# Loading the later groups' queries and keys once, two heads on 128 partitions, with the split parts written across the halves

## The chip, the cores and the metric

The kernel runs on one core of a Trainium2 chip. The metric is device microseconds of one execution, the median of several runs.

## What is computed

Causal attention with a bias that decays with the cumulated `s`, then two expert layers on its output. Cut to what matters:

```python
scores = q @ k.T / sqrt(D)                       # B, H, S, D = 2, 8, 576, 64
cum = cumsum(maximum(s, 0))
scores = where(causal, -1e9, scores + minimum(-(cum[:, None] - cum[None, :]), 0))
x = softmax(scores) @ v                          # -> 1152 tokens of 512
h = x @ w_in                                     # 512 x 2048
x = where(h > 0, h, exp(minimum(h, 0)) - 1) @ w_out
out = sum_e p[:, e] * (maximum(x @ w1[e], 0) @ w2[e])   # 4 experts, 512 x 1024
```

Everything is float32 outside. Inside, products that must be exact are made of rounded numbers (float32r): a number is split into a high part (a rounded copy, made by ScalarE) and a low part (the number less its high part, made by VectorE), and three products or, in the attention, two stacked ones give the full result.

## The kernel before

The engines are TensorE (PE), VectorE (DVE), ScalarE (ACT), GpSimd (POOL) and SyncE (SP), which issues the loads. The 1152 tokens are worked in three groups (`GROUPS`) of 256, 448 and 448 tokens. For each group there is attention, the first layer (`layer1`, 16 weight units) and the second layer (4 experts of 8 units). The attention of group 0 (`attention_first`) comes first by itself; that of groups 1 and 2 (`attention_parts`) is cut into small parts which run as `background` between the slots of the layers of the group before: group 1's beside the last slots of group 0's first layer (from slot `BG_FROM[0]`, 14) and all of its second layer, group 2's beside group 1's first layer.

A slot of the first layer (`up1`, `down1`) makes `up` products of one unit, an `e` on ACT (L721, L724), a `gt` on DVE (L725) and, two slots later, the `acc` products with it. There are two `up` buffers, so a slot's `up` products wait for the `gt` of two slots before. At the end of group 0's first layer ACT rounds the four sums to `yh` (L772), and the second layer begins with products of `yh` and `yl`.

The weights of the first layer come coded and are decoded on ACT and DVE in `decode_halves` (L150, L157, L158, L160), 32 halves; POOL writes each decoded unit to `w_dec` (L163), from which groups 1 and 2 read it again. The weights from unit 16 on are loaded into `raw` (`fetch`, L97, three buffers) and split by `prepare`: a cast on ACT (L103) and a subtraction on DVE (`split_lo`, L87). Units are numbered here in this order: unit 16 is the first of the second layer of group 0.

A job of `attention_parts` is one pair of heads (128 rows of `qT` and `kT`) with its query chunks. Group 1 has four small jobs (128 queries, batch 1), loaded together by `load_small` into one tile `pt`, and four of 320 queries and 576 keys; group 2 has four of 256 queries and 384 keys and four of 192 queries and 576 keys. These are loaded by `load`. An item is one 128-query chunk of one head. Its two products (`qk`) are

```python
PE.matmul(pss, job[j, "q"], job[j, "kh"], start=True, stop=False)    # [q high; q low] x [k high; k high]
PE.matmul(pss, job[j, "qb"], job[j, "kl"], start=False, stop=True)   # [q high; bias rows] x [k low; bias rows]
```

so `qs` and `kh` need 128 partitions of one head whose width is 64. Before, each head was therefore loaded twice, onto partitions 0 to 63 and onto 64 to 127 (`for half in range(2)`, L420 to 422 and L442 to 447), and `split` copies 128 partitions to `qs` (L478) and `kh` (L479) and lets DVE overwrite the upper half of `qs` with the low part. Chunks of 64 queries (`j is None`) take both heads at once with rows `64 * jj` of `q` and `k` (L497).

The code gives the order in which work is recorded; the framework's scheduler then fixes, when the program is built, the order on each engine, and each engine works through its own in order. Loads of the first jobs are held until the last coded half is issued (`late`). SP uses eight completion semaphores in turn, so that a load is issued once the eighth before it has landed.

Of the kernel before, what the change touches and what calls it, by code (L numbers as in the profile page):

```python
# [12 lines left out]
AF = mybir.ActivationFunctionType  # L13
# [40 lines left out]
def tile_kernel(ctx, tc, qT, kT, v, s, w64, w, probs, out):  # L54
# [13 lines left out]
    PE, DVE, ACT, POOL, SP = nc.tensor, nc.vector, nc.scalar, nc.gpsimd, nc.sync  # L68
# [6 lines left out]
    def sb(shape, tag, bufs, dtype=F32):  # L75
        p = (base if tag in BASE else edge if tag in EDGE else l1_pool if tag in L1
             else att_pool[0])
        return p.tile(shape, dtype, tag=tag, name=tag, bufs=bufs)
# [7 lines left out]
    def split_lo(lo, x, hi):  # L86
        DVE.tensor_tensor(out=lo, in0=x, in1=hi.bitcast(F32), op=ALU.subtract)  # L87
# [141 lines left out]
    def cum_rows(h0, heads, n, out_):  # L229
        return dict(  # L230
            out=out_,
            in_=cum_d[h0:h0 + heads, 0:n].rearrange("(o h) k -> o h k", o=1)
            .to_broadcast([out_.shape[0], heads, n]),
        )
# [163 lines left out]
    def attention_parts(g, x):  # L398
# [3 lines left out]
        for b, chunks, col in JOBS[g]:  # L402
            cb = CHUNKS[b]
            q0, q1 = cb[chunks[0]], cb[chunks[-1] + 1]
            for hp in range(HP):
                job = dict(b=b, chunks=chunks, col=col, q0=q0, q1=q1, hp=hp)
                full = [i for i in chunks if cb[i + 1] - cb[i] == 128]
                mine = [dict(job=job, i=i, j=j) for j in range(2) for i in full]
# [5 lines left out]
        def load_small():  # L414

            b = small[0]["b"]
            t = sb([128, 2560], "pt", 2)
            q, k = (t[:, a:a + 1024].rearrange("p (h n) -> p h n", n=128) for a in (0, 1024))
            vv = t[:, 2048:].rearrange("p (c d) -> p c d", d=128)
            for t, x in ((q, qT), (k, kT)):  # L420
                for half in range(2):
                    SP.dma_start(out=t[64 * half:64 * half + 64],
                                 in_=x[b, :, 0:128].rearrange("(h d) n -> d h n", d=64))
            SP.dma_start(out=vv.rearrange("p c d -> p (c d)"), in_=v[b, 0:128])
            pt = sb([128, HP, 2, 128], "pt", 2)
            for job in small:
                hp = job["hp"]
                job["q"], job["k"] = q[:, 2 * hp:2 * hp + 2], k[:, 2 * hp:2 * hp + 2]
                job["v"] = vv[:, hp:hp + 1]
                job["pt"] = pt[:, hp].rearrange("p j (o n) -> p j o n", o=1)  # L430

        def load(job):
            b, hp, q0, q1 = job["b"], job["hp"], job["q0"], job["q1"]
            cb, nc_ = CHUNKS[b], job["chunks"][-1] + 1
            nq = q1 - q0
            r = slice(hp * 128, hp * 128 + 128)

            def buf(shape, tag):
                return sb(shape, tag, 2)

            for n, x, a, e in (("q", qT, q0, q1), ("k", kT, 0, q1)):
                job[n] = t = buf([128, 2, e - a], n + "2")  # L442
                for half in range(2):
                    SP.dma_start(
                        out=t[64 * half:64 * half + 64],
                        in_=x[b, r, a:e].rearrange("(h d) n -> d h n", h=2),
                    )
            h0 = b * H + 2 * hp
            if any(cb[i + 1] - cb[i] == 64 for i in job["chunks"]):
                job["cump"] = t = buf([128, 1, q1], "cbp")  # L450
                for j in range(2):
                    SP.dma_start(**cum_rows(h0 + j, 1, q1, t[64 * j:64 * j + 64]))
            job["v"] = buf([128, nc_, 128], "v")
            full = [i for i in range(nc_) if cb[i + 1] - cb[i] == 128]
            if full:
                SP.dma_start(
                    out=job["v"][:, full[0]:full[-1] + 1, :],
                    in_=v[b, cb[full[0]]:cb[full[-1] + 1], r].rearrange("(c p) d -> p c d", p=128),
                )
            for i in range(nc_):  # L460
                if i not in full:
                    SP.dma_start(out=job["v"][:64, i, :], in_=v[b, cb[i]:cb[i + 1], r])

        def split(it):


            job, j = it["job"], it["j"]
            if j is None or (j, "q") in job:
                return
            q, k = job["q"][:, j], job["k"][:, j]  # L470
            qs = sb([128, q.shape[-1]], "qs", 2, F32R)
            kh = sb([128, k.shape[-1]], "kh", 2, F32R)
            qb = sb([68, q.shape[-1]], "qb", 2, F32R)
            kl = sb([68, k.shape[-1]], "kl", 2, F32R)
            h = job["b"] * H + 2 * job["hp"] + j
            SP.dma_start(out=qb[64:].bitcast(F32), in_=rows_d[h, 2:6, job["q0"]:job["q1"]])
            SP.dma_start(out=kl[64:].bitcast(F32), in_=rows_d[h, 0:4, 0:job["q1"]])
            ACT.activation(qs, q, AF.Copy)  # L478
            ACT.activation(kh, k, AF.Copy)  # L479
            split_lo(qs[64:], q[64:], qs[64:])  # L480
            ACT.activation(qb[:64], q[:64], AF.Copy)
            split_lo(kl[:64], k[:64], kh[:64])
            job[j, "q"], job[j, "qb"], job[j, "kh"], job[j, "kl"] = qs, qb, kh, kl

        def qk(it, pss, a, e):
            job, i, j = it["job"], it["i"], it["j"]
            cb = CHUNKS[job["b"]]
            qs = slice(cb[i] - job["q0"], cb[i + 1] - job["q0"])
            if j is not None:
                PE.matmul(pss[:, :e - a], job[j, "q"][:, qs], job[j, "kh"][:, a:e],  # L490
                          start=True, stop=False)
                PE.matmul(pss[:, :e - a], job[j, "qb"][:, qs], job[j, "kl"][:, a:e],  # L492
                          start=False, stop=True)
                return
            for jj in range(2):
                r = slice(64 * jj, 64 * jj + 64)
                PE.matmul(pss[r, :e - a], job["q"][r, jj, qs], job["k"][r, jj, a:e],  # L497
                          start=True, stop=True)

        norm = []  # L500
# [79 lines left out]
        def start():  # L580
            with late():
                if small:
                    load_small()
                for job in jobs[:2]:
                    load(job)
            split(items[0])
# [504 lines left out]
```

## Time and profile before

| what | value |
|---|---|
| median of 3 runs (lowest, highest) | 712.02 us (711.47, 712.31) |
| span of the profiled execution, first to last instruction | 710.5 us |
| PE busy | 695.7 us (98%) |
| DVE, ACT, POOL busy | 561.8 (79%), 366.9 (52%), 17.7 us (2%) |
| mean granted clock of PE | 0.997 |
| moved by DMA | 97.00 MB, mean 137 GB/s |

For the profiled execution the profile gives its span; the median of the runs is 1.5 us more, for what lies around the span. Busy time of PE counts from a matmul's start to its modelled end, and matmuls overlap. DVE's and ACT's share is a mean over stretches that differ: ACT is busy for 35 to 41 of every 50 us up to 300 us and for 11 to 19 after 400. The DMA engines are busy all the time up to 95 us and about half the time from there to 350.

### The profile page before, as it was taken

Reading aid. Unit: us, or ns where it says so; the run is one execution under the profiler, and the core shown is the slowest. Engines: PE = TensorE matmul, PEld = TensorE weight load, DVE = VectorE, ACT = ScalarE, POOL = GpSimd, SP = SyncE. Lnnn points to the kernel's source line nnn. Section 1 sums busy time; section 2 is a strip of 40 time slices with the busy share of each in tenths; the row PEclk is TensorE's granted clock in tenths of the full one; section 3 lists DMA queues with packets and bytes.
Section 4 is the critical chain, followed back from the end, with each engine's and each line's share of the span. In section 5 each row is a group of like instructions: output and inputs, shape, how many; then the busy total and the mean of one; then the engine's idle time right before and its main releaser. Section 6 shows DMA issues by size and latency. Waiting matters only on the chain.

```text
span 710.5 us, 10311 instructions
## 1 busy us (share of the span) xinstructions
PE 695.7 (98%) x3670; PEld 594.1 (84%) x3670; DVE 561.8 (79%) x1158; ACT 366.9 (52%) x765; POOL 17.7 (2%) x40
## 2 busy tenths in 40 slices
PE   8999899999999999999999999999999999999997
PEld 7787688887878887887899988888888888888886
DVE  7798679887868988875975469988888888888765
ACT  5897679676667777666754343322222233322320
POOL 5011000000000000000000000000000000000000
PEclk9999999999999999999999999999999999999999
DMA  8999965765674553523552000111111111111002
GB/s 301 410 391 380 318 204 179 226 206 171 185 222 149 173 174 94 161 98 102 226 178 89 1 1 0 60 60 59 60 60 59 60 60 59 60 60 59 1 0 105
DMA packets 40868, 97.00 MB, mean 137 GB/s; under 512 B 4096, under 2 KB 17616, under 8 KB 40816
## 3 DMA queue, kind: packets, MB, share of 16 engines
q1 hardware_dynamic: 38288, 87.67, 37.0%
q0 software_dynamic: 2528, 8.67, 3.0%
q8 instruction: 29, 0.48, 0.3%
q14 instruction: 23, 0.19, 0.1%
HBM read 85.32 MB, written 11.01 MB: 136 GB/s over the span
## 4 chain that ended last, share of the span: by engine, by line
PE 89%; ACT 6%; DVE 2%; DMA 2%; issue 1%; POOL 0%; ACTq 0%; DVEq 0%; POOLq 0%
PE acc L614 39%; PE up L614 17%; PE att L926 11%; PE up L926 8%; PE att L569 3%; PE att L542 3%; ACT z L157 2%; ACT wu L150 2%; DMA raw<-in_w 2%; PE att L497 1%; PE att L490 1%; PE att L492 1%; PE acc L704 1%; PE att L362 1%; PE up L717 1%
## 5 line engine op out<-in xcount | busy, mean ns | idle before, releaser
L614 PE MATMUL acc<-w,h 128*128 128x512 f32 x672 | 172.0, 392 | 0.0
L614 PEld LDWEIGHTS acc<-w,h 128*128 128x128 f32 x672 | 126.1, 188 | 23.0 <-ACT h L936 0.2
L87 DVE TENSOR_TENSOR wu<-raw,wu 128x1024 fp32r<-128x1024 f32 x64 | 78.0, 1220 | 18.7 <-ACT wu L103 18.2
L614 PE MATMUL acc<-gt,wu 128*128 128x448 f32 x384 | 87.8, 372 | 0.0
L671 DVE SCALAR_TENSOR_TENSOR ox<-acc,pr,ox 128x512 f32<-128x512 f32 x105 | 78.5, 748 | 11.4 <-PE acc L614 9.1
L936 ACT ACTIVATE h<-c 128x448 fp32r<-128x448 f32 x48 | 27.4, 573 | 111.2 <-DVE c L942 111.2
L614 PEld LDWEIGHTS acc<-gt,wu 128*128 128x128 f32 x384 | 70.1, 188 | 7.8 <-issue 2.6
L103 ACT ACTIVATE wu<-raw 128x1024 fp32r<-128x1024 f32 x64 | 67.5, 1055 | 16.7 <-PE acc L614 14.5
L926 PE MATMUL att<-S,top 128*128 128x448 f32 x288 | 66.3, 365 | 0.0
L926 PEld LDWEIGHTS att<-S,top 128*128 128x128 f32 x288 | 54.0, 188 | 6.7 <-issue 0.2
L614 PE MATMUL acc<-wu,gt 128*128 128x512 f32 x192 | 56.1, 408 | 0.0
L614 PE MATMUL up<-yh,wu 128*128 128x256 f32 x256 | 53.4, 289 | 0.0
L937 DVE SCALAR_TENSOR_TENSOR h<-c,h 128x448 fp32r<-128x448 f32 x48 | 29.8, 623 | 18.7 <-ACT h L936 18.7
L614 PEld LDWEIGHTS up<-yh,wu 128*128 128x128 f32 x256 | 41.7, 189 | 3.4 <-issue 1.5
L926 PE MATMUL up<-x2a,top 128*128 128x448 f32 x192 | 44.2, 366 | 0.0
L614 PE MATMUL up<-xa,wu 128*128 128x448 f32 x192 | 43.5, 371 | 0.0
L614 PE MATMUL up<-ox,wu 128*128 128x448 f32 x192 | 41.5, 366 | 0.8 <-DVE e L729 0.8
L721 ACT ACTIVATE e<-up 128x448 f32<-128x448 f32 (+1 forms) x48 | 23.5, 489 | 34.0 <-PE up L614 30.2
L532 ACT ACTIVATE p<-p,nm 128x384 f32<-128x384 f32 (+4 forms) x56 | 34.5, 617 | 12.3 <-DVE nm L527 11.9
L926 PEld LDWEIGHTS up<-x2a,top 128*128 128x128 f32 x192 | 35.9, 188 | 4.8 <-ACT p L951 0.6
L936 ACT ACTIVATE h<-up 128x448 fp32r<-128x448 f32 x16 | 8.8, 547 | 59.5 <-PE up L926 59.5
L614 PEld LDWEIGHTS up<-ox,wu 128*128 128x128 f32 x192 | 36.0, 188 | 4.0 <-DVE e L729 1.1
(193 smaller groups left out, 1223.8 us busy)
## 6 DMA issues: line engine op xcount, KB each, us to landing
raw<-in_w SPq DMA_DIRECT2D x38, 512.0 KB
raw<-w_dec SPq DMA_DIRECT2D x32, 512.0 KB
raw<-in_w SPq DMA_DIRECT2D x16, 1024.0 KB
w_dec<-wu POOLq DMA_DIRECT2D x16, 512.0 KB, 7.4
cd<-in_w SPq DMA_DIRECT2D x9, 512.0 KB
k<-in_kT SPq DMA_DIRECT2D x16, 288.0 KB
xa<-in_w SPq DMA_DIRECT2D x5, 512.0 KB
cbp<-cum_d SPq DMA_DIRECT2D x16, 144.0 KB
```

What stands on the lines that cost most here:

```text
L87: DVE.tensor_tensor(out=lo, in0=x, in1=hi.bitcast(F32), op=ALU.subtract)
L103: ACT.activation(t[:, 0], x, AF.Copy)
L150: ACT.activation(m, high.bitcast(F32), AF.Abs, scale=2.0 ** -112))
L532: ACT.activation(p, p, AF.Exp, bias=nm, scale=-1.0, accum_out=sm)
L542: PE.transpose(pt[:cb[c + 1] - cb[c], m, :], p[:, cb[c]:cb[c + 1]], ident)
L569: PE.matmul(o[64 * j:64 * j + 64, qs:nq], job["v"][:n, c, 64 * j:64 * j + 64], job["pt"][:n, j, c, qs:nq], start=c == 0, stop=c == n_c - 1)
L614: PE.matmul(o, a[m], b[n], start=first and i == 0, stop=last and i == 2)
L671: DVE.scalar_tensor_tensor(out=o_sb, in0=o, scalar=pr[:, i, e:e + 1], in1=o_sb, op0=ALU.mult, op1=ALU.add)
L721: ACT.activation(e, o, AF.Exp)
L926: PE.matmul(bank, tops[q][:, m, op, cs], x[:, n, c], start=first and c + i == 0, stop=c == 1 and i == 2, skip_group_check=True)
L936: ACT.activation(h[:, 0, u, cs], c, AF.Relu)
L937: DVE.scalar_tensor_tensor(out=h[:, 1, u, cs], in0=c, scalar=0.0, in1=h[:, 0, u, cs].bitcast(F32), op0=ALU.max, op1=ALU.subtract)
```

## The change

Queries and keys of a job are loaded once, as they lie in memory, with head 0 of the pair on partitions 0 to 63 and head 1 on 64 to 127. In `split`, `mine` is the half on which head `j` lies and `other` the other one. ACT writes the high parts `qs[mine]` and `kh[mine]`, DVE writes the low part of `q` into `qs[other]`, and ACT writes the high part of `k` once more into `kh[other]`, which is one ACT instruction more for each head. For head 1 the two stacked halves stand the other way round in `qs` and `kh`, which leaves the product the same; `qb` and `kl` stay on partitions 0 to 63. The tile of the small jobs shrinks from 2560 to 1536 columns. Lines from 421 on stand up to five lines higher, in the layers four.

```diff
         def load_small():
...
-            t = sb([128, 2560], "pt", 2)
-            q, k = (t[:, a:a + 1024].rearrange("p (h n) -> p h n", n=128) for a in (0, 1024))
-            vv = t[:, 2048:].rearrange("p (c d) -> p c d", d=128)
+            t = sb([128, 1536], "pt", 2)
+            q, k, vv = (t[:, a:a + 512].rearrange("p (h n) -> p h n", n=128)
+                        for a in (0, 512, 1024))
             for t, x in ((q, qT), (k, kT)):
-                for half in range(2):
-                    SP.dma_start(out=t[64 * half:64 * half + 64],
-                                 in_=x[b, :, 0:128].rearrange("(h d) n -> d h n", d=64))
+                SP.dma_start(out=t, in_=x[b, :, 0:128].rearrange("(h p) n -> p h n", p=128))
...
-                job["q"], job["k"] = q[:, 2 * hp:2 * hp + 2], k[:, 2 * hp:2 * hp + 2]
+                job["q"], job["k"] = q[:, hp], k[:, hp]
...
         def load(job):
...
-                job[n] = t = buf([128, 2, e - a], n + "2")
-                for half in range(2):
-                    SP.dma_start(
-                        out=t[64 * half:64 * half + 64],
-                        in_=x[b, r, a:e].rearrange("(h d) n -> d h n", h=2),
-                    )
+                job[n] = t = buf([128, e - a], n + "2")
+                SP.dma_start(out=t, in_=x[b, r, a:e])
...
         def split(it):
...
-            q, k = job["q"][:, j], job["k"][:, j]
+            mine, other = (slice(64 * i, 64 * i + 64) for i in (j, 1 - j))
+            q, k = job["q"][mine], job["k"][mine]
...
-            ACT.activation(qs, q, AF.Copy)
-            ACT.activation(kh, k, AF.Copy)
-            split_lo(qs[64:], q[64:], qs[64:])
-            ACT.activation(qb[:64], q[:64], AF.Copy)
-            split_lo(kl[:64], k[:64], kh[:64])
+            ACT.activation(qs[mine], q, AF.Copy)
+            ACT.activation(kh[mine], k, AF.Copy)
+            split_lo(qs[other], q, qs[mine])
+            ACT.activation(qb[:64], q, AF.Copy)
+            split_lo(kl[:64], k, kh[mine])
+            ACT.activation(kh[other], k, AF.Copy)
...
-                PE.matmul(pss[r, :e - a], job["q"][r, jj, qs], job["k"][r, jj, a:e],
+                PE.matmul(pss[r, :e - a], job["q"][r, qs], job["k"][r, a:e],
```

The scheduler moves more than the diff shows. On SP, behind the last two coded halves (`xa`), the loads of the small jobs (`pt_841`), of the next job (`q2`, `k2`, `cbp`) and of unit 16 (`raw_804`) and unit 17 (`raw_820`) stand so before:

```order
L422 DMA pt_841<-in_qT 64x8x128 x2
L422 DMA pt_841<-in_kT 64x8x128
L97 DMA raw_804<-in_w 128x1024
L422 DMA pt_841<-in_kT 64x8x128
L97 DMA raw_820<-in_w 128x1024
L424 DMA pt_841<-in_v 128x512
L444 DMA q2_848<-in_qT 64x2x320 x2
```

and so after:

```order
L421 DMA pt_841<-in_qT 128x4x128
L421 DMA pt_841<-in_kT 128x4x128
L422 DMA pt_841<-in_v 128x512
L441 DMA q2_846<-in_qT 128x320
L441 DMA k2_848<-in_kT 128x576
L446 DMA cbp_850<-cum_d_95 64x576
L97 DMA raw_804<-in_w 128x1024
L446 DMA cbp_850<-cum_d_95 64x576
L97 DMA raw_820<-in_w 128x1024
```

Unit 16 had three loads of `pt` ahead of it; now it has the two of q and k, the small jobs' `v`, the next job's q and k and half of its `cbp`. Unit 18 follows in both kernels behind the second job's loads.

On ACT, in the last slots of group 0's first layer, the order from the cast of unit 17 on was (`qs_928`, `kh_929`, `qb_930`: the third item's split; `p_906`: the first item's exponentials; `e_916`: the layer's last slot):

```order
L103 ACTIVATE wu_923<-raw_820 128x1024
L721 ACTIVATE e_815<-up_810 128x256
L724 ACTIVATE e_815<-e_815 128x256
L721 ACTIVATE e_831<-up_826 128x256
L724 ACTIVATE e_831<-e_831 128x256
L478 ACTIVATE qs_928<-pt_841 128x128
L479 ACTIVATE kh_929<-pt_841 128x128
L481 ACTIVATE qb_930<-pt_841 64x128
L532 ACTIVATE p_906,sm_909<-p_906,nm_907 128x128
L721 ACTIVATE e_916<-up_911 128x256
L724 ACTIVATE e_916<-e_916 128x256
```

and is

```order
L103 ACTIVATE wu_919<-raw_820 128x1024
L717 ACTIVATE e_815<-up_810 128x256
L720 ACTIVATE e_815<-e_815 128x256
L717 ACTIVATE e_831<-up_826 128x256
L720 ACTIVATE e_831<-e_831 128x256
L103 ACTIVATE wu_1066<-raw_878 128x1024
L528 ACTIVATE p_902,sm_905<-p_902,nm_903 128x128
L473 ACTIVATE qs_924<-pt_841 64x128
L474 ACTIVATE kh_925<-pt_841 64x128
L476 ACTIVATE qb_926<-pt_841 64x128
L478 ACTIVATE kh_925<-pt_841 64x128
L717 ACTIVATE e_912<-up_907 128x256
```

The cast of unit 18 (`raw_878`) now stands ahead of the first `p`, the third item's split and the last slot's `e`. Before, it (`raw_883`) stood behind `yh`, here on ACT as well:

```order
L772 ACTIVATE yh_1018<-acc0_526 128x256
L772 ACTIVATE yh_1018<-acc1_527 128x256
L772 ACTIVATE yh_1018<-acc2_528 128x256
L772 ACTIVATE yh_1018<-acc3_529 128x256
L799 ACTIVATE gt_1042<-up_1029 128x256
L799 ACTIVATE gt_1088<-up_1075 128x256
L481 ACTIVATE qb_954<-pt_841 64x128
L103 ACTIVATE wu_1066<-raw_883 128x1024
```

In the changed kernel the splits of the third to sixth item, four `p`, two copies of `pt` and the casts of units 18 and 19 stand ahead of `yh`.

## Rows read from the trace of the kernel before

**Rows 1.** Waits of PE, 60 to 345 us: total, times, longest.

```profile
PE up L717 <- DVE gt L725: 4.4, 2, 3.9
PE up L614 <- DVE e L729: 0.8, 1, 0.8
```

**Rows 2.** Timeline of PE: start, us, line, operation [idle before].

```profile
68.05 1.89 PE L704 MATMUL acc<-gt,wu 128*128 128x256 f32 x8
73.88 2.80 PE L717 MATMUL up<-xf,wu 128*128 128x256 f32 x8 [3.94 <-DVE gt L725]
...
79.77 1.99 PE L717 MATMUL up<-xf,wu 128*128 128x256 f32 x8 [0.48 <-DVE gt L725]
...
83.39 0.27 PE L492 MATMUL att<-kl,qb 68*128 68x128 f32 x1
...
103.53 0.44 PE L569 MATMUL att<-pt 128*64 128x128 f32 x4
```

**Rows 3.** Windows: PE, PEld, DVE, ACT, POOL busy, PEclk, DMA, GB/s.

```profile
40.00:45.00 5.00, 5.00 (x25) 4.39 (x24) 4.83 (x10) 4.97 (x11) 1.07 (x2) 1.00 1.03 421
74.90:78.30 3.40, 3.40 (x10) 2.69 (x9) 2.63 (x5) 2.50 (x6) 0.53 (x1) 0.50 1.05 300
80.00:86.00 6.00, 6.00 (x31) 5.30 (x30) 4.48 (x14) 2.73 (x10) 0.21 (x1) 1.00 1.05 362
86.00:91.00 5.00, 5.00 (x28) 4.43 (x26) 2.75 (x11) 3.38 (x12) 0.00 (x0) 1.00 1.10 260
91.00:93.00 2.00, 2.00 (x18) 1.98 (x17) 1.05 (x3) 0.90 (x3) 0.00 (x0) 1.00 1.03 383
100.00:345.00 245.00, 243.87 (x1493) 200.85 (x1493) 201.45 (x510) 176.43 (x402) 0.00 (x0) 1.00 0.54 171
```

**Rows 4.** Timeline of ACT, 70 to 92 us.

```profile
70.06 0.51 ACT L481 ACTIVATE qb<-pt 64x128 fp32r<-64x128 f32 x2 [3.63 <-DMA pt<-in_qT]
72.14 0.51 ACT L478 ACTIVATE qs<-pt 128x128 fp32r<-128x128 f32 x2 [1.57 <-DMA pt<-in_qT]
72.56 0.36 ACT L721 ACTIVATE e<-up 128x256 f32<-128x256 f32 x1
...
76.47 1.06 ACT L103 ACTIVATE wu<-raw 128x1024 fp32r<-128x1024 f32 x1 [0.87 <-DMA raw<-in_w]
...
84.20 0.39 ACT L532 ACTIVATE p<-p,nm 128x128 f32<-128x128 f32 x1
...
85.48 0.38 ACT L721 ACTIVATE e<-up 128x256 f32<-128x256 f32 x1 [0.80 <-PE up L717]
...
89.92 1.68 ACT L772 ACTIVATE yh<-acc 128x256 fp32r<-128x256 f32 x4 [0.18 <-PE acc L704]
```

**Rows 5.** Timeline of SP: the issue of unit 16.

```profile
65.41 0.51 SPq L97 DMA_DIRECT2D raw<-in_w  x1
```

**Rows 6.** DMA issues of the whole span: count, KB of each.

```profile
raw<-in_w SPq DMA_DIRECT2D x38, 512.0 KB
...
w_dec<-wu POOLq DMA_DIRECT2D x16, 512.0 KB, 7.4
...
k<-in_kT SPq DMA_DIRECT2D x16, 288.0 KB
...
cbp<-cum_d SPq DMA_DIRECT2D x16, 144.0 KB
v<-in_v SPq DMA_DIRECT2D x8, 256.0 KB
...
q<-in_qT SPq DMA_DIRECT2D x8, 160.0 KB
pt<-in_qT SPq DMA_DIRECT2D x4, 256.0 KB
...
v<-in_v SPq DMA_DIRECT2D x8, 32.0 KB
```

**Rows 7.** Groups of ACT by line and form: busy us, mean ns.

```profile
L479 ACT ACTIVATE kh<-k 128x576 fp32r<-128x576 f32 x16 | 10.8, 677 | 1.4 <-DMA k<-in_kT 1.4
```

## The prediction

> **What bounds the kernel now.** I read the page first: TensorE (PE) is busy for nearly the whole span, so a change of loads and copies can cost or gain only where PE stands still. The waits of PE between 60 and 345 us, which take in all the attention that the diff touches, say where: it waited 4.4 us in two pieces for `gt`, and the next largest wait is one of 0.8 us [rows 1]. [...] After 79.77 PE had no more such wait until 345 us: where attention runs beside the expert layers nothing is left to gain.
>
> ScalarE's (ACT's) timeline gives the cause [rows 4]. ACT works in order. After the last decodes it stood until 70.06 and again until 72.14 us for the two loads of the small jobs' queries, and the layer's own `e` (L721, which PE needs through `gt`) was queued behind those copies and began at 72.56. Then it stood once more, to 76.47, for weight unit 16 (first L103). So from 66 to 80 us the kernel waits for SyncE's (SP's) loads. SP's timeline shows that unit 16 was issued at 65.41, behind three loads of `pt` [rows 5]; by ACT's row it had landed by 76.47, after the two query loads at 70.06 and 72.14. I read from this that the loads are served in the order of issue, so that a landing time can be worked out from the KB ahead.
>
> **The change, part by part.**
>
> *Bytes.* By the issue sizes [rows 6] the small jobs lose two loads of 256 KB; each of the twelve other jobs loses one of two q loads and one of two k loads, 160 and 288 KB where they are largest. The loads fall by 26. After 100 us this is worth nothing, as PE waits for no load there [rows 1].
>
> *Copies.* Each of the 32 heads gets one more ACT copy, `kh[other]`. The copies of 64 partitions cost what those of 128 do, the width being the same: even at the widest form's 677 ns, 32 are under 22 us [rows 7]. From 100 to 345 us ACT was busy for 176 of 245 us [rows 3], so it has 69 us of room. I cost them at nothing there; without that cover the end would be 22 us later, which I exclude, since ACT's room is three times that. Before 100 us the copies are counted below. DVE does as many subtractions as before, now from one half of the partitions to the other; no row has such a form. I take them at their old price; the other end is double, which DVE would still hide: it was busy for 4.48 of the 6 us from 80 and for 201 of the 245 from 100 [rows 3].
>
> *First stand (69.9 to 73.88).* Before `e`, ACT now needs q and k, one load of 256 KB each, where it needed two q loads of 256 KB: 512 KB behind the same weights in both, so 72.1 again. Three copies instead of two then stand ahead of `e`, at 0.21 us each by the pair at 72.14 [rows 4]: +0.2 us. The other end is a load that goes faster for reaching 128 partitions: stretches of q, k and `cbp` loads on 64 partitions ran at 260 GB/s (86 to 91 us), one of weights on 128 at 383 (91 to 93) [rows 3]. The second of the two loads landed 2.08 us after the first; by that ratio two such save up to 1.3 us.
>
> *Unit 16.* SP now issues q, k, v of the small jobs, q and k of the next job and one `cbp` ahead of it: 3 x 256 + 160 + 288 + 144 + 512 = 1872 KB to its end, against 3 x 256 + 512 = 1280 [rows 6]. The 592 KB more (0.61 MB) take 1.6 us at 383 GB/s, 2.0 at the 300 of 74.9 to 78.3 us. I take 383, since most of these loads are now on 128 partitions: landing at 78.0 instead of 76.4 (ends 76.7, if the first loads also come 1.3 us sooner, and 78.4). ACT stands that much longer with `e` of the next slot behind it, so PE's second stand grows from 0.5 to about 2 us.
>
> *Unit 18: the step that decides.* Before, its cast stood behind the four `yh` copies; now it stands ahead of `e` of the layer's last slot, and SP still issues it behind all loads of the second job. From unit 16's landing to its own come 144 + 512 (unit 17) + 256 + 32 (v) + 160 + 288 + 2 x 144 + 256 + 32 + 512 = 2480 KB, or 2.54 MB [rows 6], and the decoded weights of the last two units, 512 KB each, are written in that time (1.05 MB). These 3.59 MB take 9.4 us at 383 GB/s: landing at 87.4. The ends: 85.2 (from 76.7, at 421 GB/s, the rate of 40 to 45 us) and 90.4 (from 78.4, at 300) [rows 3].
>
> From there to the first `yh` ACT has this ahead, by the order: two casts of 1.06, four `p` of 0.4, sixteen copies of 0.21, two copies of `pt` at the same, two passes of `e` at 0.4 [rows 4]: 2.1 + 1.6 + 3.4 + 0.4 + 0.8 = 8.3 us. The first `yh` comes at 95.7 instead of 89.92 [rows 4]: 5.8 us later, and the expert layer begins with it. PE has in that time done work that came later before: two second products (`kl`, `qb`), one transposition of the same width and one set of values, at most 3 x 0.27 + 0.44 us and less as matmuls overlap, taken as 0.8 [rows 2]. That leaves **+5.0 us**. It is no sum with the two stands before it: the later, longer wait takes them in. Nothing gives it back, since PE ran without gaps afterwards. What is late next are `p`, `pt` and the second job's splits on ACT behind `yh`; PE's next product waits for them for under a microsecond, about what it saves by having an item's two products side by side.
>
> The profiled execution spans 710.5 us; the median of the runs is 712.02, 1.5 more, for what lies around the span. 710.5 + 5.0 + 1.5 gives **717.0**.
>
> [...]
>
> **The rivals.**
>
> *Faster (0.14).* The loads on 128 partitions are quick enough that ACT finds unit 18 there, so no new wait comes, and the first stand shrinks. For: 260 against 383 GB/s [rows 3], and half the q and k bytes. Price: 1.3 us of the stand, less 0.2 for the copies, and the 1.7 us of half clock, if the shorter stand doesn't bring it: 2.8 us, **709.2**. It decides at about 84 us, where ACT gets to unit 18: from 70.8 on, 1360 + 2480 KB of loads and at least 1.05 MB of writes must go through in 13.2 us, or 377 GB/s without a pause. Against: the stretches there show 300, 362 and 260; only two microseconds of weights alone ran at 383.
>
> *No change (0.11).* Unit 18 lands near 85 and ACT catches up, because the items that it splits early are not split later, and the first stand gives 1 or 2 us back: **712.0**. Against: PE stood nowhere in that later stretch, so there is no wait that early splits could remove.
>
> *Slower, by what I forecast (0.75).* By the ends of unit 18's landing it gives +2.8 (85.2) to +8.0 (90.4): 714.8 to 720.
>
> That the change doesn't do what it says I leave out: the new loads and copies stand in the order.
>
> **How the numbers follow.** A measurement of this kernel tells 0.2% (1.4 us) from no change, so faster is below 710.6 and slower above 713.4. The likeliest case gives 717.0, its own range is 714.8 to 720. I let the whole range begin at 711.5, which keeps most of the no-change case and leaves out the faster one (0.14) and a tail above 720 (0.04).
>
> **What would show it.** Right: unit 16's first cast at 78 us and unit 18's near 87.5, each with ACT idle before it for a load of `raw`; PE waiting in the slots up to 97 us some 5 us longer than before; first `yh` near 95.7; from there to the end the same time as before. Wrong: a first stand of under 3 us and no half clock; unit 18's cast with no idle time before it; or waits of PE after 100 us for `kh` copies.

## The result and the profile after

The changed kernel takes 717.62 us (median of 6 runs, 716.83 to 718.68), the kernel before 712.26 us beside it (6 runs, 711.47 to 713.73): a ratio of 1.0074, with a 95% interval of 1.006 to 1.0087. The forecast was 717.0 us. The profiled execution spans 716.7 us and took 718.5 us; it is one of the slower of the six, and its excess over the median is told of below. One execution below, the profiled one of copy_on_pool (729.57 us), fell in a state in which the clock granted to PE was lower throughout (0.909 in the mean), and its profile is not read.

The waits of TensorE (PE), 60 to 345 us, that answer to [rows 1]:

```profile
engine line waited for: us in total, times, longest us
PE up L713 <- DVE gt L721: 4.8, 2, 4.5
PE att L538 <- ACT pt L553: 0.7, 1, 0.7
PE att L538 <- DVE p L503: 0.6, 2, 0.4
PE att L486 <- ACT e L717: 0.5, 1, 0.5
PE up L610 <- ACT yh L768: 0.5, 1, 0.5
PE att L488 <- DMA kl<-rows_d: 0.4, 1, 0.4
PE att L565 <- ACT pt L553: 0.4, 1, 0.4
```

The wait for `gt` is little longer than before (4.8 us against 4.4). New is a list of small waits, and the timeline of PE puts four of them between 88 and 96 us. Its stands (stretches in which PE is idle) from 66 to 97 us, for [rows 2]:

```profile
74.48 3.78 PE L713 MATMUL up<-xf,wu 128*128 128x256 f32 x8 [4.46 <-DVE gt L721]
80.74 1.99 PE L713 MATMUL up<-xf,wu 128*128 128x256 f32 x8 [0.30 <-DVE gt L721]
...
88.86 0.30 PE L486 MATMUL att<-kh,qs 128*128 128x128 f32 x1 [0.50 <-ACT e L717]
89.56 0.30 PE L488 MATMUL att<-kl,qb 68*128 68x128 f32 x1 [0.41 <-DMA kl<-rows_d]
...
92.64 0.33 PE L538 MATMUL att<-ident,p 128*128 128x128 f32 x1 [0.72 <-ACT pt L553]
...
95.65 0.38 PE L610 MATMUL up<-yh,wu 128*128 128x256 f32 x1 [0.46 <-ACT yh L768]
```

The first product of the second layer (`up<-yh`) comes at 95.65 us; before it came at 90.83:

```profile
90.83 0.47 PE L614 MATMUL up<-yh,wu 128*128 128x256 f32 x1
```

On ScalarE (ACT), for [rows 4], the rows that begin after a wait for `raw` are the casts of units 16 and 18; the first `e` (L717, at 72.81 us) has one more copy between its two passes:

```profile
73.22 0.31 ACT L473 ACTIVATE qs<-pt 64x128 fp32r<-64x128 f32 x1
73.55 0.42 ACT L720 ACTIVATE e<-e 128x256 f32<-128x256 f32 x1
...
77.44 1.06 ACT L103 ACTIVATE wu<-raw 128x1024 fp32r<-128x1024 f32 x1 [1.24 <-DMA raw<-in_w]
...
86.08 1.06 ACT L103 ACTIVATE wu<-raw 128x1024 fp32r<-128x1024 f32 x1 [2.48 <-DMA raw<-in_w]
...
95.23 1.19 ACT L768 ACTIVATE yh<-acc 128x256 fp32r<-128x256 f32 x4
```

Three windows for [rows 3] (columns as there): the half clock lasted from 72.2 to 79.0 us, 6.8 us instead of 3.4, of which PE worked 4.5 (4.56 by the exact ends of the clock's record, 72.22 and 79.04); between the landings of units 16 and 18 the DMA engines moved 351 GB/s; and from 100 to 345 us ACT was busy for 187 us instead of 176.

```profile
72.20:79.00 6.80, 4.52 (x11) 3.62 (x12) 3.28 (x7) 5.46 (x13) 0.53 (x1) 0.50 1.05 359
77.44:86.08 8.64, 8.34 (x36) 6.88 (x36) 6.03 (x14) 5.10 (x11) 0.53 (x1) 0.91 1.02 351
...
100.00:345.00 245.00, 243.91 (x1497) 201.80 (x1497) 197.53 (x489) 187.04 (x413) 0.00 (x0) 1.00 0.44 144
```

**Where the time went.** Four marks on PE's timeline divide the two profiled executions: the first products with `xa` (group 1's first layer; 216.02 us before, 219.80 after), with `ox` (group 2's; 336.43 and 340.96) and with `x2a` (the paired layer; 415.29 and 421.26), and the end. Up to `xa` the changed kernel lost 3.8 us, in group 1's layer 0.75, from `ox` to `x2a` 1.4, and after that 0.2. The first mark, before and then after:

```profile
216.02 2.60 PE L614 MATMUL up<-xa,wu 128*128 128x448 f32 x12
```

```profile
219.80 2.60 PE L610 MATMUL up<-xa,wu 128*128 128x448 f32 x12
```

### The profile page after: what moved, and what is told of

It is laid out like the page before. It is cut to its first block, busy times and chain, and to the rows that moved or that the text cites. A ratio compares the mean times of both kernels' runs of the same rounds, so it can differ in the third digit from the quotient of the medians.

```text
span 716.7 us, 10320 instructions
## 1 busy us (share of the span) xinstructions
PE 698.6 (97%) x3670; PEld 594.9 (83%) x3670; DVE 563.5 (79%) x1158; ACT 385.7 (54%) x797; POOL 17.7 (2%) x40
## 4 chain that ended last, share of the span: by engine, by line
PE 85%; ACT 6%; DVE 3%; DMA 3%; SPq 1%; issue 1%; POOL 0%; DVEq 0%; ACTq 0%; POOLq 0%
PE acc L610 38%; PE up L610 16%; PE att L922 11%; PE up L922 8%; PE att L565 3%; PE att L538 3%; DMA raw<-in_w 2%; ACT z L157 2%; ACT wu L150 2%; PE att L493 1%; PE att L486 1%; PE att L488 1%; PE att L362 1%; SPq L422 1%; DMA kl<-rows_d 1%
## 5 line engine op out<-in xcount | busy, mean ns | idle before, releaser
L667 DVE SCALAR_TENSOR_TENSOR ox<-acc,pr,ox 128x512 f32<-128x512 f32 x105 | 78.5, 748 | 11.4 <-PE acc L610 9.1
L610 PEld LDWEIGHTS acc<-wu,gt 128*128 128x128 f32 x192 | 32.8, 189 | 7.0 <-issue 2.5
```

The source lines that it names most:

```text
L610: PE.matmul(o, a[m], b[n], start=first and i == 0, stop=last and i == 2)
L667: DVE.scalar_tensor_tensor(out=o_sb, in0=o, scalar=pr[:, i, e:e + 1], in1=o_sb, op0=ALU.mult, op1=ALU.add)
```

## The experiments

The edits use two orders that the framework knows: `keep_in_program_order` lets the scheduler put an instruction ahead of nothing that stands before it in the code on its engine, and `issue_after` queues instructions of one engine behind a given one. Times are medians; the ratio behind each is to runs of the kernel before beside it on the same chip, whose medians were 712.69 to 713.04 us. A table for all is at the end of this section.

### Is it the cast of unit 18, the loads or the copies?

**hold_cast.** The casts of units 18 and 19 go back behind `yh`:

```diff
-        ACT.activation(t[:, 0], x, AF.Copy)
+        cast = ACT.activation(t[:, 0], x, AF.Copy)
+        if n in (NAB + 2, NAB + 3):
+            tc.keep_in_program_order(cast)
```

> The changed kernel, with the casts of units 18 and 19 kept on ScalarE behind the four yh copies, where the kernel before has them. Theory A (order): the 5 us come from that cast, which stands ahead of the layer's last e and waits for a load. Then the stand of 2.5 us at 84 to 86 us goes, the first yh comes at 90.5 to 92 instead of 95.2, and the time is 712.5 to 714. Theory B (late loads): unit 18 lands late wherever its cast stands and holds the second layer up instead: 716 to 718. Theory C (the 32 further copies of kh): 717 to 718, as nothing is taken from them.

716.86 us, ratio 1.0074 (1.0052 to 1.0097): no gain, so theory A fell as it stood. ACT's wait of 2.48 us is gone; PE has another in its place. First SyncE (SP), then PE:

```profile
79.81 2.77 SPq L97 DMA_DIRECT2D raw<-in_w  x3
84.42 0.27 SPq L473 DMA_DIRECT2D qb<-rows_d  x1
84.73 0.33 SPq L474 DMA_DIRECT2D kl<-rows_d  x1
```

```profile
87.77 0.41 PE L488 MATMUL att<-kh,qs 128*128 128x128 f32 x1
90.14 0.30 PE L490 MATMUL att<-kl,qb 68*128 68x128 f32 x1 [1.97 <-DMA kl<-rows_d]
...
94.65 0.38 PE L612 MATMUL up<-yh,wu 128*128 128x256 f32 x1
```

The bias rows of the third item could be issued only when the first item's product had freed one of two buffers, at 84.7 us, and by then three units of weights, 1.5 MB, had been issued ahead of them. They were there at 90.1. In the order before, that item's second product stood behind the first `up<-yh`; now it stands ahead of the layer's last products, and PE began these at 90.28, behind it. In the changed kernel itself the wait for the cast hid most of this one: 0.41 us were left of it. Nor did theory B hold as put, although its number came out: PE waited for unit 18's cast for 0.35 us only, and that behind other work of ACT, not for its load.

**early_cast.** The kernel before, with only that cast moved ahead of the layer's last `e`:

```diff
-        ACT.activation(t[:, 0], x, AF.Copy)
+        casts[n] = ACT.activation(t[:, 0], x, AF.Copy)
...
-        while prepare_at[0] <= min(n + 2, n_units - 1):
+        while prepare_at[0] <= min(n + (4 if n == NAB - 2 else 2), n_units - 1):
...
-                ACT.activation(e, o, AF.Exp)
+                ahead = casts.get(NAB + 2) if g == 0 and k == NAB - 1 else None
+                with tc.issue_after(ahead.ins) if ahead else nullcontext():
+                    ACT.activation(e, o, AF.Exp)
```

> The kernel before, with its old loads and copies, but with the cast of unit 18 put ahead of the e of the layer's last slot. Theory A (order): unit 18 is issued at 88.4 us here, so its cast begins at 92 to 93.5, the first yh comes at 97 to 100, and the time is 718 to 722. Theory B (late loads): the loads are those of before, so 712 to 713. Theory C (copies): no copy is added, 712 to 713.

720.21 us, 1.0112 (1.0091 to 1.0133). An order alone, with the old loads and copies, costs as much as theory A said. With the cast the scheduler also drew the second products of the third and fourth item ahead of `yh`, so in these instructions it has the order of the changed kernel on both engines. PE's stands:

```profile
94.94 0.45 PE L492 MATMUL att<-kl,qb 68*128 68x128 f32 x1 [5.42 <-DMA kl<-rows_d]
96.85 1.22 PE L704 MATMUL acc<-gt,wu 128*128 128x256 f32 x2 [1.46 <-DVE gt L727]
101.60 0.39 PE L614 MATMUL up<-yh,wu 128*128 128x256 f32 x1
```

Again two waits stand side by side. The one for `kl` covers most of the other: unit 18 landed at 94.14 us, and 1.46 us of the wait for `e` behind its cast were left over.

**copy_on_pool.** GpSimd makes the further copies:

```diff
-            ACT.activation(kh[other], k, AF.Copy)
+            POOL.tensor_copy(kh[other], k)
```

> The changed kernel, with the 32 copies kh[other] made by GpSimd instead of ScalarE; unit 18's cast still stands ahead of the last e. Theory A (order): the stand for unit 18 stays, first yh at 94 to 95.5, and only the waits of PE for p near 230 to 236 us (0.6 us) go: 716 to 717.5. Theory B: the same. Theory C (copies): 711 to 713.

717.01 us, 1.0065 (1.0045 to 1.0084), as A and B said: taking the copies off ACT doesn't bring the 5 us back (against theory C). That GpSimd's copies cost time of their own in some other place is not excluded by this run; early_cast, which has no such copy, speaks for the order.

**weights_first.** Units 16 to 18 are loaded ahead of the attention:

```diff
-        while fetch_at[0] <= min(n + 4, n_units - 1):
+        while fetch_at[0] <= min(n + (5 if n < NAB else 4), n_units - 1):
...
-            return tc.issue_after(last_coded[0].ins) if g == 1 else nullcontext()
+            return tc.issue_after(last_fetch[0].ins) if g == 1 else nullcontext()
```

> The changed kernel, with the loads of units 16 to 18 issued ahead of all loads of the attention of group 1. Theories A and B: unit 16 is there by 70 to 71 us, unit 18 by 74, the first stand of PE shrinks by 1 to 1.5 us, the second one goes, the half clock may stay away, the first yh comes at 88 to 90.5, and the time is 708.5 to 711.5, below both kernels. Theory C (copies): at least 715, as the copies stay.

713.42 us, 1.0011 (1.0001 to 1.0021): 4 us better than the changed kernel, with the same smaller loads and further copies (so theory C fell), and still above the 708.5 to 711.5 that A and B said and not below the kernel before. Its waits of PE, 60 to 216 us:

```profile
PE up L713 <- DVE gt L721: 2.1, 1, 2.1
PE att L565 <- ACT pt L553: 1.0, 2, 0.6
PE att L486 <- DVE sm L502: 1.0, 1, 1.0
PE att L486 <- ACT kh L478: 0.7, 1, 0.7
PE up L610 <- DVE yl L87: 0.6, 1, 0.6
PE att L486 <- ACT pt L553: 0.5, 1, 0.5
```

The stand for `gt` was halved and the half clock stayed away, as expected. What was not expected are some 4 us of further waits, most of them of the attention's products, which now meet their own late inputs.

### Two waits side by side?

**rows_queue** and **rows_queue_hold.** GpSimd issues the rows on its own queue, in the second with the casts held as in hold_cast:

```diff
-            SP.dma_start(out=qb[64:].bitcast(F32), in_=rows_d[h, 2:6, job["q0"]:job["q1"]])
-            SP.dma_start(out=kl[64:].bitcast(F32), in_=rows_d[h, 0:4, 0:job["q1"]])
+            POOL.dma_start(out=qb[64:].bitcast(F32), in_=rows_d[h, 2:6, job["q0"]:job["q1"]])
+            POOL.dma_start(out=kl[64:].bitcast(F32), in_=rows_d[h, 0:4, 0:job["q1"]])
```

> The changed kernel, with the 4-row loads of rows_d into qb and kl issued by GpSimd on its own queue instead of SyncE's; the order on ScalarE and TensorE stays, unit 18's cast ahead of the last e. Theory D (two waits side by side: unit 18's cast on ScalarE, and the third item's kl rows, which were issued behind three units of weights and landed near 89.5 to 90 us): with the rows early the cast alone still holds the layer up, so only the 0.4 us wait of kl goes, and the time is 716.3 to 717.8. Theory A (the cast alone): the same. Theory E (the rows alone, since holding the cast back gave nothing): 712.5 to 714.

717.66 us, 1.0059 (1.0039 to 1.008). The wait for `kl` went and PE stood 1.31 us for `e` in its place: the cast alone holds the layer up as well. Theory E fell.

> The same, and the casts of units 18 and 19 held behind the yh copies as well. Theory D: both waits are gone, the 2.0 us wait of TensorE for kl at 90 us does not come, first yh product at 92 to 93.5 us (the products and copies pulled ahead of it remain, and the first stand is 0.5 us longer), 713.5 to 715. Theory F (no wait counts; the lost time is the attention work that stands ahead of yh in the order): 716 to 717.5, as with the cast held back alone.

719.25 us, 1.0083 (1.006 to 1.0107): worse, against theory D's number, because the edit did not do what it was for. GpSimd's row and PE's:

```profile
85.49 0.52 POOL L474 DMA_DIRECT2D kl<-rows_d  x1
```

```profile
91.56 0.45 PE L490 MATMUL att<-kl,qb 68*128 68x128 f32 x1 [3.32 <-DMA kl<-rows_d]
```

PE's product began 6.1 us after the issue of the 2 KB it waited for; three units of weights had been issued on SP's queue from 80.10 us on. And GpSimd's queue wasn't free either: `w_dec`'s last write, 512 KB, was issued on it at 80.47 us, and the sixteen such writes of this run took 7.5 us in the median:

```profile
80.47 0.53 POOL L165 DMA_DIRECT2D w_dec<-wu  x1 [3.75 <-DVE wu L162]
```

Which of the two held the rows up, no run here separates. With this stand came a half clock (granted clock 0.50) from 90.9 to 97.7 us: four `acc` products took 2.02 us at 91.81, where four took 1.08 at 87.10.

**four_buffers_hold.** As hold_cast, with four buffers for `qb` and `kl`, so that the third item's rows are issued ahead of the large loads:

```diff
-            qb = sb([68, q.shape[-1]], "qb", 2, F32R)
-            kl = sb([68, k.shape[-1]], "kl", 2, F32R)
+            qb = sb([68, q.shape[-1]], "qb", 4, F32R)
+            kl = sb([68, k.shape[-1]], "kl", 4, F32R)
```

> The changed kernel, with four buffers instead of two for qb and kl, so that the third item's rows are issued ahead of the attention's large loads, and with the casts of units 18 and 19 held behind the yh copies. Theory D (two waits side by side, unit 18's cast and the third item's kl rows): neither is left ahead of yh, so no wait of TensorE of over 1 us between 82 and 95 us, first yh product at 92 to 93 us, 713 to 715. Theory F (the attention work that stands ahead of yh costs the time, not a wait): 716.5 to 718.

717.6 us, 1.0073 (1.0059 to 1.0086): the number that theory F gave. The waits are as theory D said; PE's, 60 to 216 us:

```profile
PE up L715 <- DVE gt L723: 5.7, 2, 4.6
PE up L612 <- ACT wu L103: 0.6, 1, 0.6
PE att L540 <- ACT pt L555: 0.3, 1, 0.3
```

In the profiled execution, which was the fastest of the six (716.51 us), the first `xa` product came 1.5 us earlier than in the changed kernel. But the first two stands are 1.3 us longer than before's 4.4, and group 1's layer lost another 1.0 us (table). So in the profile removing both waits is worth 1.5 us up to `xa`, and the median doesn't show it. Theory F has a part in it too: the first `yh` product came at 93.20 us, 2.4 us behind before, where the stands up to there are only 1.5 us longer and the half clock is shorter; about a microsecond is attention work that now stands ahead of it, most of which is saved again by `xa`.

### Can the stretch be freed of waits?

**weights_first_late** and **weights_first_late_old.** weights_first with `BG_FROM[0]` at 16 instead of 14, and the same two edits on the kernel before.

> The changed kernel, with units 16 to 18 loaded ahead of all attention loads and the attention of group 1 started two slots later (16 instead of 14), so that no item of it stands ahead of the layer's last slots. Theory D: weights_first shortened the stands (3.0 us against 5.6) and gave it back in waits of the attention's products (4 to 5 us between 79 and 94 us); without these 707.5 to 710.5. Rival: the attention, started later, runs out of room before group 1's layer at 216 us and waits there: 712 to 715.

> The same two edits on the kernel before, with its old loads and copies. Theory D: with the weights out of the way the loads of the attention no longer decide, so it stands within 1 us of weights_first_late, either side: the change itself is worth nothing there. Rival: the fewer bytes help once nothing waits behind them, so this is 2 us or more above weights_first_late.

718.16 us, 1.0063 (1.0039 to 1.0087), and 718.13 us, 1.0065 (1.0044 to 1.0086): equal to each other, as D said, and both some 8 us above the top of its range (and above the rival's). By then five units stood ahead of the attention on SP, the last two waiting for buffers, so `pt` landed at 82.65 us with the layer's last `e` behind its splits. Four waits of 0.5 to 1.4 us between 84 and 92 us followed, and with them this window:

```profile
87.60:97.80 10.20, 8.64 (x33) 7.10 (x33) 8.27 (x29) 7.33 (x25) 0.00 (x0) 0.50 0.39 106
```

10.2 us at half clock, 8.6 of them work, cost 4.3 us, about what the shorter first stand and the full clock had brought in weights_first.

**casts_last.** The attention starts at slot 17, behind unit 18's load; four buffers; the casts of units 16 and 17 and the small jobs' splits are kept behind every `e` of the layer:

```diff
-BG_FROM = [14, 0, 0]
+BG_FROM = [17, 0, 0]
...
+        if n < NAB + 2:
+            tc.keep_in_program_order(cast)
...
-        while prepare_at[0] <= min(n + 2, n_units - 1):
+        while prepare_at[0] <= min(n + (0 if n == NAB - 2 else 2), n_units - 1):
...
+            pin = tc.keep_in_program_order if job in small else lambda i: i
+            pin(ACT.activation(qs[mine], q, AF.Copy))
```

> The changed kernel, with units 16 to 18 loaded ahead of the attention, the casts of units 16 and 17 and the small jobs' splits kept on ScalarE behind every e of the first layer, the attention started three slots later (17) and four buffers for qb and kl. If the time is the sum of TensorE's stands between 66 and 100 us and of half the time at half clock (theory G), then e never waits for a load, both stands of before (4.4 us) and its half clock (1.7 us) go, first yh product near 84 to 86 us, 705.5 to 708.5. Rival: the waits come back at the first attention products or at units 18 to 20, whose loads now stand behind all of the attention's: 710 to 714, with waits of wu or kh between 88 and 105 us.

716.79 us, 1.0061 (1.0047 to 1.0074). PE ran through the whole stretch from 66 to 82 us without a stand, the first time in these kernels. Then a wait came after all, and the time lies outside both ranges: not for weights or `kh`, as the rival had it, but on VectorE (DVE) for a load, and so on PE for `gt`:

```profile
83.90 0.49 DVE L241 TENSOR_SCALAR bias<-cbp,cum_p 128x512 f32<-128x512 f32 x1 [7.38 <-DMA cbp<-cum_d]
```

```profile
84.97 3.12 PE L703 MATMUL acc<-gt,wu 128*128 128x256 f32 x8 [2.87 <-DVE gt L724]
```

The scheduler had drawn a job's bias ahead of the layer's last `gt`, and it stood there for `cbp`.

**no_early_waits** and **no_early_waits_old.** As casts_last with two buffers and both bias instructions of `add_bias` kept in program order as well; and all these edits on the kernel before.

> As casts_last but with two buffers for qb and kl, and the bias of the 64-query chunks kept on VectorE where it is recorded: in casts_last it stood ahead of the layer's last gt and waited for cbp from 76.5 to 83.9 us. Theory G (the time is TensorE's stands between 66 and 110 us, half the time at half clock, and the waits for p in group 1's layer): no stand of over 1.5 us up to the first yh product, which comes at 83.5 to 85.5 us, and no half clock; some 2 us of waits of the attention's products up to 125 us and 0.8 us in group 1's layer stay: 709.5 to 712.5, 0 to 3 us below before. Rival: another load that stands late in the order takes the place, 714 to 717.

> The same edits on the kernel before, with its old loads and copies. Theory G: no stand ahead of yh either, and without the 32 further copies nothing is lost in group 1's layer: 709 to 711.5, some 0.8 us below no_early_waits. Rival (the fewer bytes help): 2 us or more above no_early_waits.

713.86 us, 1.0013 (1.0002 to 1.0023), and 716.72 us, 1.0052 (1.0039 to 1.0064). The first `yh` product of the former came at 83.79 us, 7 us ahead of before, and then units 19 and 20, whose loads stood behind the attention's, took it back. ACT, then PE:

```profile
89.32 1.06 ACT L103 ACTIVATE wu<-raw 128x1024 fp32r<-128x1024 f32 x1 [3.42 <-DMA raw<-in_w]
```

```profile
83.79 0.33 PE L615 MATMUL up<-yh,wu 128*128 128x256 f32 x1
...
91.96 1.96 PE L615 MATMUL acc<-wu,gt 128*128 128x512 f32 x4 [3.77 <-ACT gt L800]
```

So theory G's number fell: another late load took the place, as the rival said, at 713.86 us just below its 714 to 717, and with it came a half clock from 92.1 to 95.5 us (3.4 us in the table below). Between the two kernels G's sign fell as well: with the same edits the new loads are 2.9 us better by the medians. In the old one ACT waited 1.33 us for the second `pt` load of keys and `yh` behind it; in the new one that load was there. This is less than half of the 2.9 us; the scheduler's orders of the two differ in more than these loads, and what the rest is stays open.

### One account for all

The columns: median; PE still between 60 us and the first `xa` product; PE busy at half clock in that time; the first `xa` product; from there to the first `ox` product; from there to the first `x2a` product. All but the first are of the profiled execution, from PE's rows and granted clock.

| kernel | median | still | at half clock | xa | to ox | to x2a |
|---|---|---|---|---|---|---|
| before | 712.26 | 4.4 | 3.4 | 216.0 | 120.4 | 78.9 |
| changed | 717.62 | 7.3 | 4.6 | 219.8 | 121.2 | 80.3 |
| hold_cast | 716.86 | 7.8 | 3.4 | 219.7 | 121.2 | 78.9 |
| early_cast (old) | 720.21 | 11.4 | 8.6 | 224.5 | 120.2 | 78.9 |
| weights_first | 713.42 | 6.3 | 0.0 | 216.2 | 121.2 | 78.9 |
| rows_queue | 717.66 | 8.0 | 4.5 | 221.3 | 121.3 | 78.9 |
| rows_queue_hold | 719.25 | 9.5 | 9.6 | 223.7 | 121.3 | 78.9 |
| weights_first_late | 718.16 | 5.9 | 8.7 | 220.5 | 121.2 | 80.3 |
| weights_first_late_old | 718.13 | 7.3 | 11.6 | 222.5 | 120.2 | 78.9 |
| four_buffers_hold | 717.60 | 6.7 | 2.9 | 218.3 | 122.1 | 78.9 |
| casts_last | 716.79 | 5.7 | 3.3 | 218.0 | 122.2 | 80.3 |
| no_early_waits | 713.86 | 4.8 | 3.4 | 216.6 | 121.4 | 78.9 |
| no_early_waits_old | 716.72 | 6.6 | 3.4 | 219.6 | 120.2 | 78.9 |

This is an account of the profiles, not an experiment. Half of the time is taken because the products took twice as long there: in the changed kernel eight `up` products took 3.78 us at 74.48, at a granted clock of 0.50, and 1.89 at 66.40, at 1.00. Still time plus half of the time at half clock, taken off the `xa` column, leaves 208.9 to 211.3 us in all thirteen. For the changed kernel against the one before it is (7.3 + 2.3) - (4.4 + 1.7) = 3.4 of the 3.8 us. So, to within 1.2 us, what these kernels lose or win ahead of `xa` is stands and slow clock, nearly all of it between 66 and 118 us; the rest of group 0 takes the same time in all within that.

The column to `ox` splits by the change alone: the four kernels with old loads and copies take 120.2 to 120.4, the nine with new ones 121.2 to 122.2, the two above 122 being those with four buffers.

No version is faster than the kernel before.

## Why the prediction was right, and where not

**The first stands: right.** The two query and key loads landed at 69.76 and 71.96 us, and `e` began at 72.81 instead of 72.56: +0.25 us for +0.2. What was left out is a copy (L473, 73.22 us) between its two passes: the second began at 73.55 instead of 72.95, and PE's stand ended 0.60 us later (74.48 for 73.88).

**Unit 16: right in the landing, wrong in what it does.** 77.44 us for 78.0, inside 76.7 to 78.4. But PE's second stand shrank to 0.30 us where about 2 were forecast. `gt` came 0.97 us later, as the landing says, but PE came to it 1.15 us later: 0.60 by the first stand and 0.57 by the longer half clock (4.56 us of work at it instead of 3.41), which the forecast left as it was.

**Unit 18: landing and size right, the verdict "decides" wrong.** It landed at 86.08 us, inside 85.2 to 90.4. But both terms behind it were mis-sized, with opposite signs. The rate from unit 16's landing to unit 18's was 351 GB/s where 383 was taken, and in the 8.64 us the engines moved 3.03 MB where 3.59 were counted: 2.24 on SP's queue for 2.54, and 0.78 on GpSimd's for the 1.05 of the two `w_dec` writes. So loads that were issued behind unit 16 had moved in part before it landed, and the last write was not through: a landing here does not follow from the KB issued ahead alone. Nor did the first two loads gain by the ratio of 260 to 383 GB/s that the first stand's other end was worked out from: on 128 partitions the second landed 2.20 us after the first, on 64 it was 2.08. No run measured loads on 64 and on 128 partitions by themselves. From the cast to `yh` it took 9.15 us for 8.3. So `yh` came at 95.23 on ACT for 95.7, since a landing that was 1.3 us sooner than forecast and a path from the cast to `yh` that was 0.9 us longer nearly cancel: luck, in part. But hold_cast shows that this wait decides nothing alone: without it the third item's `kl` rows hold PE up, and rows_queue shows the reverse. The step looked for what is late next behind `yh` only, and put it at under a microsecond; the `kl` rows stand ahead of `yh`, and PE waited 1.97 us for them once the cast was held back. I had followed the order of one engine, ACT, to its wait, and not PE's order to the loads that its own products need.

**What is given back: wrong.** From the `yh` product to `xa` the lag fell from 4.8 to 3.8 us; 0.8 had been allowed off ACT's 5.8, and off its measured 5.3 it was 1.5.

**Copies after 100 us at nothing: wrong by 0.75 us.** "From there to the end the same time" did not hold. The copies' price held (64x576 in 670 and 675 ns for the 677 of 128x576) and ACT's room was there (187 of 245 us busy), but a chain of waits can run through it. In the changed kernel's group 1 layer the further copy (L478) stands ahead of a cast and of `p`; ACT, then PE:

```profile
231.55 0.51 ACT L478 ACTIVATE kh<-k 64x384 fp32r<-64x384 f32 x1
232.08 1.06 ACT L103 ACTIVATE wu<-raw 128x1024 fp32r<-128x1024 f32 x1
233.04 0.60 ACT L528 ACTIVATE p<-p,nm 128x384 f32<-128x384 f32 x1
```

```profile
235.47 0.52 PE L538 MATMUL att<-ident,p 128*128 128x128 f32 x3 [0.42 <-DVE p L503]
```

That the loss goes with the change is shown by the table's `ox` column; that it is this copy rather than the loads is argued from these rows. They explain a part at most: between `xa` and `ox` PE's idle time grew from 0.35 to 0.72 us, less than half of the 0.75, and what the rest is stays open.

**The total.** +3.8 up to `xa` and +0.75 behind make 4.5 us, where the forecast had 5.0 and nothing. And the 5.0 was one long stand behind unit 18's cast, while 3.4 of the 3.8 came in pieces: 0.5 in the first stand, less 0.2 in the second, 2.5 in six small ones from 88 to 110 us, and 0.6 of half clock. The medians differ by 5.4. In the profiled execution 1.4 us more came between `ox` and `x2a`, which comes and goes with executions and not with the change (below); where the median's other 0.8 us lie is not shown. So the direction and the place were right for their reason, the order of loads and casts, and that the total came within 0.6 us is in part luck.

**The rivals.** "Faster" failed at its own condition: unit 18 was not there at 84 us, and from 71.96 to 86.08 us the engines moved 353 GB/s where it needed 377. The 1.7 us of half clock in its price are half of the 3.40 us that PE worked at 0.50 [rows 3]; in the changed kernel it worked 4.56 us at it. What it saw in the smaller loads may be there: under other orders the new loads were 2.9 us better in one pair of twins (no_early_waits) and equal in the other (weights_first_late). "No change" failed as well: nothing was caught up before `yh`, whose first product came 4.8 us later.

## What to carry to other kernels

When a change moves the order, follow each in-order engine to every load that it will now meet, the second latest too: here two waits ended within a microsecond of each other, and taking away either gained nothing clear of the noise. In this stretch, where the transfers were busy all the time (DMA share 1.03 from 71.96 to 86.08 us in the changed kernel), reorderings passed the stand on to another load (`kl` in hold_cast, `cbp` in casts_last, `raw` in no_early_waits): of these versions one (weights_first) won back most of what was lost, and none went below the kernel before. The price of a version ahead of `xa` was here, to within 1.2 us, the sum of the stands and of half the time at half clock, read off the matmul engine's timeline. And spare time of an engine is cover only where its instructions may be late: 69 us of room on ACT did not keep group 1's layer from losing 0.75 us, in part, by the rows, through a copy ahead of a `p` that PE was about to need.

## What the hardware showed

**Half clock came beside small waits as well as beside a large one.** A stand of 3.94 us was followed by 3.4 us at a granted clock of 0.50 [rows 2, 3], one of 4.46 us came with a piece of 6.8 us at 0.50 that began inside it. In weights_first_late the clock fell at 87.6 us, after stands of 0.84 and 1.40 us, and stayed at half for 10.2 us, while weights_first, with a stand of 2.12 us and several up to 1.0, kept the full clock (table: 0.0 us at half). What lowers it is not shown.

**A small transfer issued on another engine's queue was not quick beside large ones:** in rows_queue_hold PE's product began 6.1 us after the issue of the 2 KB it waited for on GpSimd's queue, with a write of 512 KB issued 5.0 us ahead on that queue and 1.5 MB of weights on SP's; over the run, the 16 transfers of 9 KB on the same queue took 2.0 us in the median.

**The same products ran 2% slower for 75 us in some executions.** In group 2's first layer PE waits once, 0.8 us in both kernels, and yet a unit's 24 products took 4.96 us in the changed kernel's profile and 4.87 in before's. The same DVE row of successive units, before and then after:

```profile
376.48 0.62 DVE L87 TENSOR_TENSOR gt<-e,gt 128x448 fp32r<-128x448 f32 x1 [0.64 <-ACT gt L732]
381.35 0.63 DVE L87 TENSOR_TENSOR gt<-e,gt 128x448 fp32r<-128x448 f32 x1 [0.65 <-ACT gt L732]
```

```profile
376.67 0.63 DVE L87 TENSOR_TENSOR gt<-e,gt 128x448 fp32r<-128x448 f32 x1 [0.64 <-ACT gt L728]
381.63 0.63 DVE L87 TENSOR_TENSOR gt<-e,gt 128x448 fp32r<-128x448 f32 x1 [0.64 <-ACT gt L728]
```

PE's rows show products every 206.7 ns there instead of 202.7 on average, at a granted clock of 1.00. The stretch takes 78.9 or 80.3 us and nothing between (table), in 3 of 13 profiled executions the latter. It is probably part of the spread of 1.8 us among the six runs; what sets it stays open.
